# Windowed attention into a channel mix on one core: how the first batch's q and k come in, where its bias is added, how masks are stored, and a new order of all instructions

## The chip, the cores and the metric

The kernel runs on one core of one Trainium2 chip. The core has TensorE (PE, matrix products and transposes into PSUM), VectorE (DVE), ScalarE (ACT), GpSimd (POOL) and SyncE (SP). DMA transfers are issued here from SP (plain copies and transposing copies) and from POOL (copies that also cast fp32 to bf16). The metric is device time in microseconds (us), less is better; the time of a kernel is the median of its runs.

## The reference

q, k, v are fp32 arrays of 8 batches x 8 heads x 576 positions x 64. Attention is causal with a window of 128 positions and a linear distance bias per head; its result, with the heads side by side (512 columns), goes through a channel mix with a hidden width of 1024.

```
scores = scale * q @ k.T
bias   = slopes[h] * -(i - j)            # slopes 2^-1 ... 2^-8
mask   = (i - j >= 0) & (i - j < 128)
attn   = softmax(where(mask, scores + bias, -1e9));  y = attn @ v
x      = y as (batch, position, 512);  x_prev = x shifted by one position
xk = mu_k*x + (1-mu_k)*x_prev;  xr = mu_r*x + (1-mu_r)*x_prev
out = sigmoid(xr @ w_r) * (relu(xk @ w_k)**2 @ w_v)
```

Inputs and output are fp32; the kernel computes in bf16 with fp32 accumulation.

## The kernel before

**Units of work.** Heads are handled in pairs: pair `it` is batch `it // 4`, heads `2*(it%4)` and the next; there are 32. A pair has scores in two halves (`score.it.e`): the transposed k is the weight, and a half is one PSUM buffer of 2 heads x 512 columns that holds, for key blocks of 128, only the 256 query columns within reach. ACT takes the exponential of a half (`exp`), `av` multiplies by v with a column of ones beside it (so that it also gives the sum), DVE divides (`norm`), and the result is transposed (`ot`, `xt`) into x with channels on partitions. `xk` and `xr` are the two mixes. The channel mix works on column chunks of two batches (P = 0 to 3): `m1` (w_k), `rl` (relu on ACT), `kk` (square), `m2a`/`m2` (w_v, in two halves of the hidden width), `m3` (w_r), `rs` (tanh), `oo` (product) and `st` (store).

**Distance and mask.** For the pairs 0 to 3 (`EARLY`, batch 0) the bias is added in PSUM: two matmuls per half (line 206) multiply a scaled identity `sid` by the matrix of distances `dist` before the score's own matmuls add to it; positions outside the window have a distance of at least 2^20. For all other pairs the exponential is multiplied on DVE by a stored `mask` (line 246), which is the exponential of the bias, made on ACT from `dist` for two heads at a time (`mask0`). Both `dist` and `mask` hold 512 columns per head: 256 made directly, and 256 copied from them (`dcopy`, `mcopy`), in the layout of the second half of a pair.

**q and k of batch 0.** Pair 0's come in fp32 by two plain loads on SP (`lq`) and are cast on DVE (`c`, line 143), which also brings two heads beside each other. Pair 1's come by two casting loads on POOL (`lqp`), those of pairs 2 and 3 by two more (`lql`), and DVE reorders each pair (`ct`, line 157). Then PE transposes (`tq`, `tk`, line 166), and ACT copies q (`pq`) and DVE k (`pk`) out of PSUM. Batches 1 to 4 come by casting loads on POOL and `ct`; batches 5 to 7 are transposed by DMA (`tr`, `trt`).

**What sets the order.** Every operation is declared with its dependences, and the table `ORDER` names for each engine the order of its instructions. A small planner only interleaves these lists; each engine runs its own list strictly in order, and an instruction that waits holds all behind it. Rings bound how far one kind may run ahead: two score buffers (`sa`), four other PSUM buffers (`mm`), three relu buffers (`rl`). On POOL the loads and the clearing of buffers are one list, and the transfers behind its issues are served one after the other. PE starts with eight warm-up matmuls on zeros (line 190), and three more groups of 5, 2 and 3 (`fill`) stand in its list, the groups of 5 and 3 ahead of `tq.0`.

**Squares.** `kk` runs on DVE (line 341) except for two of the eight column groups of the hidden width in most chunks (`KFO`, `KCH`), 16 in all, which run on ACT (line 338).

Of the kernel before, what the change touches and what calls it, by code (L numbers as in the profile page):

```python
# [16 lines left out]
def kernel(  # L17
# [107 lines left out]

    def load_qp(g, i):
        nc.gpsimd.dma_start(
            out=ql_buf[0][:, g // 2, i, 2 * (g % 2):2 * (g % 2) + 2],
            in_=(q, k)[i][0, 2 * g:2 * g + 2, 0:SM].rearrange("h (p r) d -> p h (r d)", p=128))
# [57 lines left out]
    def warm(n):
        ps = p_mm.tile([128, 512], FP32, tag="mm", name="wm")
        for _ in range(n):
            nc.tensor.matmul(ps, lhsT=zero[:, 0:128], rhs=zero, start=True, stop=True)  # L190
# [4 lines left out]

    def scores(it, e):
# [4 lines left out]
        a0 = BASE[pieces[0][0]] + pieces[0][1] - 128 * pieces[0][0]  # L201
        w = sum(n for _, _, n in pieces)
        sa = T["sa", it, e] = p_sa.tile([128, 2, 512], FP32, tag="sa", name="sa")
        if early:
            for hl in range(2):
                nc.tensor.matmul(
                    sa[:, hl, 0:w] if e else sa[:, hl, 0:w].rearrange("p (u c) -> p u c", u=2),
                    lhsT=sid[:, 2 * g + hl],
                    rhs=dist if e else dist[:, None, 0:256].to_broadcast([128, 2, 256]),
                    start=True, stop=False, skip_group_check=True)  # L210
# [820 lines left out]
```

## Time and profile before

| | |
|---|---|
| time, three runs | 231.13 us median (230.84 to 231.31) |
| profiled execution, first to last instruction | 230.5 us |
| PE busy | 222.2 us (96%) |
| DVE busy | 192.2 us (83%) |
| ACT busy | 155.4 us (67%) |
| POOL busy | 88.7 us (38%) |
| chain that ended last, share on PE | 84% |
| DMA | 33.65 MB moved, mean 146 GB/s |

The page gives the span of one execution, and no other time for that execution; the runs' median is 0.6 us above that span. A line of a group or of the timeline reads: start, duration (in the timeline), engine, line of the kernel, operation, tile written <- tiles read, shapes, count, and in brackets how long the engine stood idle before it and what ended that. A busy PE is not a PE at its peak, since matmuls overlap and their ends are modelled.

### The profile page before, as it was taken

What the parts mean: (1) busy time and instruction counts of PE and PEld (TensorE: products, weight loads), DVE (VectorE), ACT (ScalarE), POOL (GpSimd) and SP (SyncE); (2) the same over time, 40 slices, a digit from 0 to 9 for tenths busy, and PEclk for the clock granted to TensorE, in tenths of its full rate; (3) what the DMA queues carried; (4) which work ended last, traced back from release to release, by engine and by line L of the source; (5) the groups of instructions that cost most, each with busy time, mean ns of one, the idle gap of its engine ahead of it and who ended that gap; (6) DMA issues with size and microseconds to landing.
All of it is one profiled execution on the core that took longest, in us unless ns stands there. A gap on an engine that the chain in (4) does not pass through costs nothing.

```text
span 230.5 us, 5326 instructions
## 1 busy us (share of the span) xinstructions
PE 222.2 (96%) x2099; PEld 130.0 (56%) x2099; DVE 192.2 (83%) x409; ACT 155.4 (67%) x265; POOL 88.7 (38%) x127
## 2 busy tenths in 40 slices
PE   7889899999999999999999999899999999999994
PEld 2446577855685565456657554455574555456653
DVE  7577999999998998999798996996876998985252
ACT  4299999985999998783789555685168744226700
POOL 8987857563897000697001954540000000000000
PEclk9999999999999999999999999999999999999999
DMA  6999999999999986999996999999954252413014
GB/s 137 160 173 187 198 177 192 195 180 162 177 155 161 154 120 100 123 128 204 120 256 144 166 120 156 203 176 197 134 128 119 79 163 77 102 46 141 0 67 162
DMA packets 117305, 33.65 MB, mean 146 GB/s; under 512 B 99608, under 2 KB 112928, under 8 KB 117280
## 3 DMA queue, kind: packets, MB, share of 16 engines
q0 software_dynamic: 83600, 16.52, 92.3%
q1 hardware_dynamic: 33680, 16.79, 34.1%
q8 instruction: 16, 0.26, 0.4%
q14 instruction: 9, 0.07, 0.1%
HBM read 33.56 MB, written 9.44 MB: 187 GB/s over the span
## 4 chain that ended last, share of the span: by engine, by line
PE 84%; ACT 7%; DMA 4%; DVE 2%; issue 1%; SPq 0%; DVEq 0%
PE pv L364 25%; PE ps L326 25%; PE pr L349 13%; PE sa L262 7%; PE sa L229 6%; DMA tt<-ts 4%; PE wm L190 3%; PE tp L166 3%; ACT at L237 3%; ACT qk L146 2%; PE pv L371 2%; ACT xt L287 1%; PE tp L282 1%; DVE qk L143 1%; ACT rl L332 1%
## 5 line engine op out<-in xcount | busy, mean ns | idle before, releaser
L237 ACT ACTIVATE at<-sa 128x1024 bf16<-128x1024 f32 x64 | 64.7, 1043 | 14.3 <-PE sa L229 14.2
L326 PE MATMUL ps<-xk,wk_sb 128*128 128x256 bf16 (+2 forms) x416 | 73.2, 314 | 0.5 <-DVE xk L315 0.4
L332 ACT ACTIVATE rl<-ps 128x256 bf16<-128x256 f32 (+2 forms) x104 | 46.3, 482 | 37.0 <-PE ps L326 30.0
L364 PE MATMUL pv<-wv_sb,kk 128*128 128x512 bf16 x272 | 65.3, 379 | 0.0
L326 PEld LDWEIGHTS <-wk_sb 128*128 128x128 bf16 x416 | 38.5, 98 | 24.1 <-issue 2.4
L364 PEld LDWEIGHTS <-kk 128*128 128x128 bf16 x272 | 25.5, 98 | 28.4 <-issue 1.3
L246 DVE TENSOR_TENSOR at<-at,mask 128x1024 bf16<-128x1024 bf16 x56 | 37.4, 684 | 1.9 <-ACT at L237 1.9
L118 POOL DMA_DIRECT2D vs<-in_v_dram x32 | 28.5, 897 | 26.3 <-PE sa L262 16.1
L341 DVE TENSOR_TENSOR kk<-rl 128x256 bf16<-128x256 bf16 (+2 forms) x88 | 28.0, 335 | 10.3 <-ACT rl L332 10.1
L349 PE MATMUL pr<-wr_sb,xr 128*128 128x512 bf16 x144 | 36.0, 379 | 0.0
L379 DVE SCALAR_TENSOR_TENSOR ot<-rs,pv 128x512 f32<-128x512 bf16 (+1 forms) x38 | 24.4, 653 | 7.4 <-PE pv L364 5.8
L315 DVE SCALAR_TENSOR_TENSOR xk<-dl,mu_sb,xt 128x576 bf16<-128x576 bf16 (+2 forms) x36 | 27.1, 752 | 1.3
L315 DVE SCALAR_TENSOR_TENSOR xr<-dl,mu_sb,xt 128x576 bf16<-128x576 bf16 x32 | 25.5, 812 | 0.0
L355 ACT ACTIVATE rs<-pr 128x512 bf16<-128x512 f32 x36 | 21.5, 608 | 4.9 <-PE pr L349 4.6
L262 PEld LDWEIGHTS <-at 128*128 128x128 bf16 x576 | 21.6, 98 | 5.3 <-issue 0.4
L274 DVE TENSOR_TENSOR xu<-sa,rc 128x640 bf16<-128x640 f32 x28 | 23.1, 824 | 1.2 <-DMA xt<-xu 0.3
L146 ACT COPY qk<-tp 128x1024 bf16<-128x1024 bf16 (+1 forms) x20 | 18.9, 960 | 5.6 <-PE tp L166 4.6
L349 PEld LDWEIGHTS <-xr 128*128 128x128 bf16 x144 | 13.2, 98 | 12.6 <-issue 0.4
L90 POOL DMA_DIRECT2D ql<-in_k_dram x12 | 10.9, 919 | 23.0 <-DVE ct L157 21.1
L262 PE MATMUL sa<-vs,at 128*128 128x65 bf16 x448 | 18.9, 194 | 0.0
L308 DVE TENSOR_TENSOR dl<-xt 128x576 bf16<-128x576 bf16 (+2 forms) x36 | 15.1, 420 | 3.2 <-DMA xt<-xu 2.1
L229 PE MATMUL sa<-qk 64*128 64x256 bf16 (+1 forms) x160 | 13.2, 259 | 0.8 <-ACT qk L146 0.5
(70 smaller groups left out, 207.6 us busy)
## 6 DMA issues: line engine op xcount, KB each, us to landing
out_dram<-ot SPq DMA_DIRECT2D x34, 256.0 KB, 3.6
vs<-in_v_dram POOLq DMA_DIRECT2D x32, 128.0 KB, 8.0
ql<-in_k_dram POOLq DMA_DIRECT2D x9, 256.0 KB, 6.7
ql<-in_q_dram POOLq DMA_DIRECT2D x9, 256.0 KB, 7.3
ql<-in_k_dram POOLq DMA_DIRECT2D x13, 128.0 KB, 6.5
ql<-in_q_dram POOLq DMA_DIRECT2D x13, 128.0 KB, 7.6
wk_sb<-in_moe_w_k_dram POOLq DMA_DIRECT2D x2, 512.0 KB, 9.0
wv_sb<-in_moe_w_v_dram POOLq DMA_DIRECT2D x2, 512.0 KB, 8.5
```

Source lines behind the costliest of these rows:

```text
L118: nc.gpsimd.dma_start(out=vs_buf[b % NLD][:, j, :, 0:D], in_=v[b, :, 128 * j:128 * j + 128, :].rearrange("h p d -> p h d"))
L229: nc.tensor.matmul(to, lhsT=kk_, rhs=qq_, start=not early, stop=True, skip_group_check=True)
L237: nc.scalar.activation(out=at_half(it, e), in_=T.pop(("sa", it, e)), func=AF.Exp, scale=float(scale))
L246: nc.vector.tensor_tensor(out=at, in0=at, in1=m, op=ALU.mult)
L262: nc.tensor.matmul(pa[:, hl, W * (t - t0):W * (t - t0) + W], lhsT=at[:, lo:lo + 128], rhs=vs[:, u, 2 * g + hl, :] if u < NF else tvb[:, 2 ...
L315: nc.vector.scalar_tensor_tensor(out=to, in0=T["dl", it][:, c0:c1], scalar=mu_sb[:, NPO * which + g:NPO * which + g + 1], in1=xp, op0=ALU. ...
L326: nc.tensor.matmul(ps[:, 0:c1 - c0], lhsT=wk_sb[:, po, 128 * fo:128 * fo + 128], rhs=xk[:, po, c0:c1], start=(po == 0), stop=(po == NPO - 1))
L332: nc.scalar.activation(out=rl[:, 0:c1 - c0], in_=T.pop(("ps", P, c0, fo))[:, 0:c1 - c0], func=AF.Relu, scale=RELU_SCALE)
L341: nc.vector.tensor_tensor(out=T["kk", P, c0][:, fo, 0:c1 - c0], in0=rl[:, 0:c1 - c0], in1=rl[:, 0:c1 - c0], op=ALU.mult)
L349: nc.tensor.matmul(pr, lhsT=T["xr", P][:, po, 128 * c:128 * c + 128], rhs=wr_sb[:, po], start=(po == 0), stop=(po == NPO - 1))
L364: nc.tensor.matmul(pv, lhsT=kk[:, fo, o:o + 128], rhs=wv_sb[:, fo], start=(fo == 0), stop=(fo == NFO - 1))
L379: nc.vector.scalar_tensor_tensor(out=T["ot", P, c][:, w0:w1], in0=T["rs", P, c][:, w0:w1], scalar=1.0, in1=pv[:, 0:w1 - w0], op0=ALU.add, ...
```

## The change

1. All eight loads of q and k of batch 0 are plain fp32 loads on SP (`lq`, `NHW = 4`), into both buffers that the DMA transposes use later. Each is cast once (`c`), straight into the order that the transposes read; three of the casts are on ACT, five on DVE. The four casting loads on POOL and the three `ct` of batch 0 go. q and k are transposed and copied apart for each of the four pairs.
2. The two bias matmuls of a half become an operation of their own (`bias`) with a place of its own in PE's list. It takes the score's PSUM buffer and waits for `sid` alone.
3. `dist` and `mask` hold 320 columns: 64 for distances counted from 0 on, and then the 256 as before. The second half reads them by a pattern whose rows overlap (`both`), and the copies `dcopy` and `mcopy` go. The key blocks of the second half lie in another order (`BASE`), and a block of padding columns behind each `at` buffer goes, with its memsets. A mask waits only for its own two heads' `mask0`.
4. `sid` is made on POOL, ahead of all loads there; the memsets and clears come ahead of the loads too.
5. The filler groups on PE are 2 and 2 instead of 5, 2 and 3.
6. The engine of an operation is read from `ORDER` (`flex`): 49 squares are on ACT instead of 16, of the PSUM copies of q and k `pq.0`, `pq.1`, `pq.2`, `pq.19` go to DVE and `pk.1` to ACT, `xt.0.0` and `xt.11` go to DVE, `tcopy.3` to ACT.
7. All five order lists are new. A branch that scaled x on ACT, used by no pair, is taken out.

```
-    KFO, KCH = (1, 5), ((0, 512), (0, 768), (1, 0), (1, 512), (1, 896), (2, 0), (2, 512), (2, 896))
-    XMUL = ()
-    NHW = 1
+    NHW = 4
...
-    ldr = qt_buf[-1].rearrange("p i j g c -> p (i j g c)").bitcast(FP32)[
-        :, 0:4 * NHW * NF * D].rearrange("p (i g h c) -> p i g h c", i=2, g=NHW, h=2)
+    ldr = [t.rearrange("p i j g c -> p (i j g c)").bitcast(FP32).rearrange(
+        "p (g i h c) -> p g i h c", g=2, i=2, h=2) for t in qt_buf]
+    cs0 = ql_buf[0].rearrange("p w i h c -> p (w i h c)").rearrange(
+        "p (g i r h d) -> p g i r h d", g=G, i=2, r=NF, h=2)
...
     def load_qk(g, i):
         nc.sync.dma_start(
-            out=ldr[:, i, g],
+            out=ldr[g // 2][:, g % 2, i],
...
     def cast_qk(g, i, f):
-        if i == 0:
-            T["cs", g] = csp.tile([128, 2, NF, 2, D], BF16, tag="ct", name="cs")
-        f(T["cs", g][:, i].rearrange("p r h d -> p h r d"),
-          ldr[:, i, g].rearrange("p h (r d) -> p h r d", d=D))
+        f(cs0[:, g, i].rearrange("p r h d -> p h r d"),
+          ldr[g // 2][:, g % 2, i].rearrange("p h (r d) -> p h r d", d=D))
...
-    BASE = (0, 256, 512, 768, 960)
+    BASE = (0, 256, 768, 576, 512)
...
+    LT = 64
+    NK = LT + 256
+
+    def both(t, o, step, n):
+        rows = t[:, 0].ap if n > 1 else t.ap
+        return bass.AP(t.tensor, t.offset + o, [list(rows[0]), [step, n], [LT, 2], [1, 256]])
+
+    def bias(it, e):
+        g = it % G
+        sa = T["sa", it, e] = p_sa.tile([128, 2, 512], FP32, tag="sa", name="sa")
+        for hl in range(2):
+            nc.tensor.matmul(
+                sa[:, hl].rearrange("p (u c) -> p u c", u=2),
+                lhsT=sid[:, 2 * g + hl],
+                rhs=both(dist, 0, 320, 1)[:, 0] if e else
+                dist[:, None, LT:].to_broadcast([128, 2, 256]),
+                start=True, stop=False, skip_group_check=True)
...
     def masked(it, e):
         g = it % G
-        at, m = at_half(it, e), mask[:, 2 * g:2 * g + 2]
+        at = at_half(it, e).rearrange("p h (u c) -> p h u c", u=2)
         if e == 0:
-            at = at.rearrange("p h (u c) -> p h u c", u=2)
-            m = m[:, :, None, 0:256].to_broadcast([128, 2, 2, 256])
+            m = mask[:, 2 * g:2 * g + 2, None, LT:].to_broadcast([128, 2, 2, 256])
+        else:
+            m = both(mask, 2 * g * NK, NK, 2)
...
     def square(P, c0, c1, fo):
-        if fo in KFO and (P, c0) in KCH:
+        if ENGOF.get(("kk", P, c0, fo)) == "ACT":
...
+        for c0, n in ((LT, 256), (0, LT)):
+            nc.gpsimd.iota(dist[:, c0:c0 + n], pattern=[[1, n]], base=0, channel_multiplier=-1,
+                           allow_small_or_imprecise_dtypes=True)
...
-    def make_sid(h):
-        nc.vector.tensor_scalar(out=sid[:, h], in0=ident,
+    def make_sid(h, eng):
+        eng.tensor_scalar(out=sid[:, h], in0=ident,
                                 scalar1=-(2.0 ** (-(h + 1))) / scale,
                                 scalar2=None, op0=ALU.mult)
...
+    def flex(name, eng, busy, run, deps=(), pri=0, alloc=None, uses=()):
+        eng = ENGOF.get(name, eng)
+        f = {"ACT": act_cast, "DVE": vec_cast, "POOL": pool_cast}[eng]
+        return op(name, eng, busy, lambda: run(f), deps, pri, alloc, uses)
...
-    FILL = (5, 2, 3)
+    FILL = (2, 2)
```

The beginnings of the new lists:

```
PE    tk.0 fill.0 fill.1 tq.0 tq.3 tk.3 bias.0.0 score.0.0 bias.3.0 tq.1 tk.1 tk.2 score.3.0 bias.1.0 tq.2
      bias.2.0 score.1.0 av.0.0 av.3.0 tmu score.2.0 tail.0 bias.2.1 score.2.1 ot.0.0 av.2.0 bias.3.1 av.1.0
      ot.3.0 score.3.1 ot.2.0 bias.0.1 ot.1.0 tq.7 bias.1.1 score.0.1 score.1.1 tq.5 tq.4 av.0.1 av.2.1 tail.1
      score.4.0 av.3.1 tq.6 ot.2.1 ot.0.1 score.7.0 av.1.1 ot.3.1 score.6.1 m1a.0.0.0 m1a.0.0.1 m1.0.0.0
      m1.0.0.2 m1.0.0.1 ot.1.1 score.5.0 m1.0.0.4 m1.0.0.6 m1.0.0.5 ...
ACT   mask0.6 mask0.2 c.0.0 c.3.1 mask0.4 pq.3 c.1.1 exp.0.0 pk.1 exp.3.0 mask0.0 exp.1.0 exp.2.0 exp.2.1
      exp.3.1 xt.3.0 xt.1.0 pq.7 exp.0.1 xt.2.0 pq.5 pq.4 exp.1.1 exp.4.0 pq.6 xt.2.1 xt.0.1 xt.3.1 exp.6.1
      exp.7.0 rl.0.0.2 xt.1.1 rl.0.0.0 rl.0.0.1 exp.5.0 ...
DVE   c.0.1 c.3.0 id8 pk.0 pq.0 c.1.0 pk.3 c.2.1 pq.1 c.2.0 pq.2 pk.2 norm.0.0 tcopy.0 norm.3.0 cmu xt.0.0 ...
POOL  sid ms clear clear0 lvs.0.0 lvs.0.1 lts.0.1 lts.0.0 lql.1.1.0 lql.1.1.1 lql.1.0.1 lql.1.0.0 lvs.0.4
      lvs.0.3 lvs.0.2 lts.1.1 lts.1.0 lts.2.0 lwk.0 lts.2.1 lwk.1 lvs.1.3 lql.2.1.1 lvs.1.0 lql.2.1.0 lvs.1.1
      lvs.1.4 lvs.1.2 lql.2.0.0 lql.2.0.1 lwr lql.3.1.1 lql.3.1.0 lts.3.0 lts.3.1 lwv.0 lwv.1 ...
SP    lq.0.1 lq.0.0 lq.3.0 lq.3.1 lq.1.0 lq.1.1 lq.2.1 lq.2.0 lmu.0 lmu.1 ...
```

More of the change, by code (lines that the diff above doesn't have):

```diff
@@ L200, in scores @@
         pieces = HALVES[e]
-        a0 = BASE[pieces[0][0]] + pieces[0][1] - 128 * pieces[0][0]
-        w = sum(n for _, _, n in pieces)
-        sa = T["sa", it, e] = p_sa.tile([128, 2, 512], FP32, tag="sa", name="sa")
+        a0 = 512 * e
         if early:
[L205 to L210, printed above, removed]
+            sa = T["sa", it, e]
+        else:
+            sa = T["sa", it, e] = p_sa.tile([128, 2, 512], FP32, tag="sa", name="sa")
         for (u, q0, n) in pieces:
@@ L906, in memsets_early @@
     def memsets_early():
-        for i in range(NAT):
-            nc.gpsimd.memset(at_buf[i][:, 2048:2112], 1.0)
         for i in range(2):
@@ L924, in add_qk @@
                [("tr", b - 2, 0), ("tr", b - 2, 1)] if b - 2 in CROSSED else
-               [("ct", G * (b - 2) + 2 * w + j) for j in range(2)]
-               if b > 2 or b == 2 and w else [], dma=dma[i], land=min(b, 2) * 700)
+               [("ct", G * (b - 2) + 2 * w + j) for j in range(2)] if b > 2 else
+               [(t, g) for t in ("tq", "tk") for g in range(2 * w, 2 * w + 2)] if b == 2 else [],
+               dma=dma[i], land=min(b, 2) * 700)
     def add_tails(b):
@@ L981 @@
         add_pair(it)
-    for i in range(2):
-        op(("mcopy", i), "DVE", (700, 270)[i], lambda i=i: copy_mask(i),
-           [("mask0", h) for h in range(0, H, 2)], 7 * G)
     for b in range(1, B):
```

471 lines of the change are left out of this document (215 added, 256 removed).

## The prediction

> **What bounds the kernel now.** I read the head of the page first, then the busy time by stretches.
>
> ```profile
> span 230.5 us, 5326 instructions
> PE 222.2 (96%) x2099; PEld 130.0 (56%) x2099; DVE 192.2 (83%) x409; ACT 155.4 (67%) x265; POOL 88.7 (38%) x127
> ```
>
> ```profile
> core 0: us, PE busy (x) PEld busy (x) DVE busy (x) ACT busy (x) POOL busy (x), PEclk, DMA share, GB/s
> 0.00:12.00 12.00, 9.97 (x51) 4.38 (x52) 7.70 (x26) 4.67 (x8) 11.07 (x27) 1.00 1.21 150
> 12.00:30.00 18.00, 16.06 (x232) 10.62 (x232) 15.00 (x43) 17.86 (x31) 14.85 (x25) 1.00 1.62 188
> 30.00:60.00 30.00, 29.90 (x339) 20.00 (x337) 29.69 (x65) 25.82 (x46) 17.63 (x24) 1.00 1.88 186
> 60.00:80.00 20.00, 20.00 (x231) 13.21 (x230) 18.44 (x40) 18.89 (x34) 13.39 (x16) 1.00 1.80 144
> 140.00:210.00 70.00, 69.21 (x546) 37.02 (x545) 59.62 (x115) 38.45 (x68) 6.81 (x8) 1.00 0.93 137
> ```
>
> From 30 us on PE hardly idles: 0.10 us to 60 and 0.79 in the stretch 140 to 210. Nothing large can be won there. The first 30 us are different: PE's 9.97 of 12 is mostly filler, ACT does 4.67 of 12 and then 17.86 of 18. So the opening is where time lies, and in it ACT, which is late to start and then full. The timeline of the opening, engine by engine:
>
> ```profile
> 1.19 6.44 PE L190 MATMUL wm<-zero 128*128 128x512 bf16 x16 [1.19 <-DVE zero L448]
> 7.47 0.39 PE L166 MATMUL tp<-ident,cs 128*128 128x128 bf16 x4
> 28.68 1.16 PE L326 MATMUL ps<-xk,wk_sb 128*128 128x256 bf16 x9
> ...
> 9.73 1.02 ACT L237 ACTIVATE at<-sa 128x1024 bf16<-128x1024 f32 x1 [1.25 <-PE sa L229]
> 16.34 1.93 ACT L237 ACTIVATE at<-sa 128x1024 bf16<-128x1024 f32 x2
> 26.32 1.06 ACT L146 COPY qk<-tp 128x1024 bf16<-128x1024 bf16 x1
> 27.21 1.09 ACT L237 ACTIVATE at<-sa 128x1024 bf16<-128x1024 f32 x1
> 28.75 0.49 ACT L332 ACTIVATE rl<-ps 128x256 bf16<-128x256 f32 x1
> ...
> 3.61 0.78 DVE L143 CAST cs<-qt 128x512 bf16<-128x512 f32 x1 [0.56 <-DMA qt<-in_q_dram]
> 4.38 0.60 DVE L143 CAST cs<-qt 128x512 bf16<-128x512 f32 x1
> 9.32 0.80 DVE L157 COPY ct<-ql 128x1024 bf16<-128x1024 bf16 x1
> ```
>
> The reader is to see three dates. The first transposes start at 7.47 though both casts were done by 5.0: sixteen fillers stood ahead of them. The second pair starts at 9.32, when its loads have come. The first relu starts at 28.75, and with it w_k's matmuls run without gaps (28.68). Ahead of that relu ACT runs eleven exps, the copies of seven pairs and eight copies of x.
>
> **The loads.** Here are size and landing of the second plain load, then POOL's queue: its second issue, the first load behind its opening memsets, the second half of w_k, w_v's issues; and the landing times of lines 138 (its first two), 436 and 441.
>
> ```profile
> qt<-in_k_dram SPq DMA_DIRECT2D x1, 256.0 KB, 3.1
> ...
> 2.24 0.76 POOL L138 DMA_DIRECT2D ql<-in_q_dram  x1
> 4.05 0.70 POOL L127 DMA_DIRECT2D ql<-in_k_dram  x1
> 17.65 0.74 POOL L436 DMA_DIRECT2D wk_sb<-in_moe_w_k_dram  x1 [0.78 <-DMA vs<-in_v_dram]
> L441 POOL DMA_DIRECT2D wv_sb<-in_moe_w_v_dram x2: 763/763/763, 34.3 to 36.3; - x2
> ...
> DMA to landing us min/median/max: 6.5/6.7/7.0
> DMA to landing us min/median/max: 8.5/9.0/9.6
> DMA to landing us min/median/max: 8.0/8.5/9.0
> ```
>
> The first plain load lands at 3.6 (the wait of its cast) and the second, 3.1 after its issue, by 4.38 (its cast starts without a wait): 0.75 apart. Eight of them in the new order (k0, q0, q3, k3, q1, k1, k2, q2) then land at 3.6, 4.35, 5.1, 5.85, 6.6, 7.35, 8.1, 8.85: the last one before pair 2 and 3's loads of now (2.24 + 7.0 = 9.24). On POOL, the queue now moves, between the landings at 9.24 and 17.65 + 9.6 = 27.25, the two loads of pair 1 (256 KB), batch 0's v and tails (704), batch 1's q, k and tails (1152) and w_k (1024): 3136 KB by the tiles' sizes in 18.0 us, 174 KB/us. On SP the two loads of mu now stand behind eight loads, three microseconds later; tmu, which wants them, is behind the first av.
>
> **POOL's new opening.** It issues no q or k of batch 0 (four issues of 0.7 to 0.9 us gone, 768 KB), but does a second iota, sid, the small memsets and all clears before its first load. Costs of groups by shape:
>
> ```profile
> L460 POOL MEMSET tt<- 128x256 bf16 x1 | 0.4, 394 | 0.0
> L908 POOL MEMSET at<- 128x64 bf16 x4 | 0.5, 208 | 0.0
> L428 ACT ACTIVATE mask<-dist 128x256 bf16<-128x256 bf16 x8 | 2.8, 408 | 0.6 <-DVE dist L415 0.6
> L146 ACT COPY qk<-tp 128x512 bf16<-128x512 bf16 x4 | 2.3, 584 | 4.9 <-PE tp L166 3.9 <-DVE qk L143 0.8
> L143 DVE COPY qk<-tp 128x512 bf16<-128x512 bf16 x4 | 2.8, 689 | 2.6 <-PE tp L166 2.5
> L338 ACT ACTIVATE kk<-rl 128x384 bf16<-128x384 bf16 x6 | 3.2, 538 | 0.0
> L341 DVE TENSOR_TENSOR kk<-rl 128x384 bf16<-128x384 bf16 x26 | 8.9, 352 | 7.1 <-ACT rl L332 7.0
> L246 DVE TENSOR_TENSOR at<-at,mask x56: 674/684/694, 32.6 to 192.0; 128x1024 bf16<-128x1024 bf16 x56
> ```
>
> A tensor_scalar on POOL does not occur. Nearest are its memsets, 208 ns for 64 columns and 394 for 256. Eight of 128 columns lie between 1.7 and 3.2 us; I take 2.5, and for an unknown stall up to double that. The clear of one batch takes the 1.05 us between 3.00 and 4.05; three of them and the small memsets make some 3.7 (estimate). So the first v load is issued at 1.5 + 2.5 + 3.7 = 7.7, say 8.0. It lands 2.9 us later (like a plain load) to 6.5 (like the first cast load); I take 4, so 12.0. Behind it, up to the second half of w_k, stand 2880 KB: 16.6 us at 174, so 28.6 against 27.25 now. For w_v's second half: 45.3 now; in the new order 3776 KB follow w_k, and between 27.25 and 45.3 the queue moved 3328 KB (184 KB/us), so 28.6 + 20.5 = 49.1. All weights come 1.4 to 3.8 us later than now; the price is what PE wants of them, below.
>
> [...]
>
> **The path to the first relu.** PE: eight warm-ups, tk.0, four fillers instead of ten. At the row's pace (1.19 to 7.47 for sixteen, 0.39 each, early ones slower) tq.0 starts at 6.7 instead of 7.47. DVE then runs pk.0, pq.0 (0.69 each, second done 7.9), c.1.0, pk.3, c.2.1, pq.1, c.2.0 (0.6 to 0.69 each) to 11.1, and pq.2, pk.2 to 12.9. ACT gets masks 6 and 2 (four activations; width 320 makes 408 at most 510 ns), c.0.0 at 4.4, c.3.1 at 5.85, pq.3 and c.1.1 (a cast on ACT has no row: the PSUM copy's 0.584 is nearest, 0.4 to 0.8 the bounds) and starts the first exp at 8.65 (9.73 now). The next ones follow at 10.25, 12.2 and, when pk.2 is done, 13.5: four exps end at 14.4, where the fourth now ends at about 17.3 (the pair at 16.34). score.2.1 needs tcopy.0, whose tail lands at about 13.6; exp.2.1 at 15.2. From there ACT has no wait: seven exps at 0.96, four copies at 0.89 (26.32 to 27.21) and six xt at about 0.3 make 12.3, first relu at **27.5** instead of 28.75. pq.6 is then done too.
>
> Does PE profit? Useful work by the chain's pieces:
>
> ```profile
> 34.82 0.45 PE tp L166 x8
> 39.25 0.55 PE sa L262 x18
> 47.62 3.45 PE pv L364 x16
> 51.07 0.55 PE sa L229 x12
> ```
>
> A pair's eight transposes are 0.45, its av 0.55, its two score halves 0.55, a 512-column matmul 0.216. Before 28.68 PE now has done seven pairs' transposes (3.15), sixteen bias matmuls (3.45), thirteen score halves (3.6), four av (2.2), tails and x transposes (1.55), one unit of w_k (0.43): 14.4. In the new list m1.0.0.4 is the first to want both a PSUM buffer behind the first relus (about 28.65) and w_k's second half (28.6). Ahead of it stand eight pairs' transposes (3.6), the same bias, av and tails, twelve halves (3.3) and three units (1.3): 15.4. PE is **1.0 us ahead** at the same date. Bias matmuls on their own cost nothing more: same sixteen, same width. They take the score's buffer earlier (there are two): bias.1.0 waits for the first exp (9.65), bias.2.0 for the second (11.2), and behind them on PE stand score.1.0 and score.2.0, whose operands come at 11.1 and 12.9 anyway; with earlier operands that wait would be the next one.
>
> **The rest.** 33 squares go from DVE to ACT (12 of 256, 12 of 384, 9 of 512 columns). On the row of 384: 352 off DVE, 538 on ACT; in all some 11 us less DVE, 17 us more ACT, hidden by ACT's 75 us of idle time, except that ACT has only 1.1 us free of 20 in 60 to 80. Two DVE copies of the masks and one of dist go. [...] Of PE's idle 0.89 us after 30 some may go and some may come, since every list is new: I take 0.2 saved, bounds 0.9 saved and 0.8 lost. The last units, products and stores keep their form, so the tail is the same.
>
> Sum: the profiled execution's 230.5 minus 1.0 minus 0.2 is 229.3. What lies around the span is not in the page; the median of the runs is 231.13, 0.6 more, so **229.9**.
>
> **Rivals.** *More gain.* POOL's opening at its lower bounds (1.7 for sid, 2.9 to land) brings w_k 1.9 us earlier, and relieved DVE lets PE follow: 229.9 - 1.9 = 228.0. For it: DVE's 29.69 of 30 in 30 to 60. Against it: ACT is as full.
>
> *Nothing gained.* The lead is taken back at w_v: m2a.0.1 comes about 17 us of PE work after m1.0.0.4, 45.6, and the first half lands at 46.3, the second at 49.1 against 48.3. PE in order waits 0.7 to 0.9 there: 231.0. Against it: PE would have to run that stretch at full density, which now it does not.
>
> *Slower, by POOL.* Sid on POOL at double (5 us) and 6.5 to the first landing put all cast loads 5 us later at the worst; I price 3 us. Then m1.0.0.4 waits for w_k until 31.6, PE cannot pass it, and 3.0 - 1.2 remain: 232.9; it decides from about 1.2 us late. For it: no row of such work on POOL, and no load is issued before sid. Against: the memset rows.
>
> *Slower, by ACT.* The moved squares fall into 30 to 80, where ACT has 5.3 us free (50 minus 44.71): some 5 us more work there delays relus, PSUM comes free late, PE waits 2 us: 231.9. Against: DVE loses as many squares.
>
> *Slower, by the clock.* Sixteen matmuls took 6.28 us at the start, where the later 0.216 would make 3.46: PE opens at about half pace. If with six fillers fewer it stayed so from 7 to 13.4, its 4.2 us of work there would take 8.4, 2 us too many: 231.9. [...]
>
> **Chances.** Forecast 0.40 (its own range 229.2 to 230.6), more gain 0.20, nothing gained 0.18, POOL 0.12, ACT 0.07, clock 0.03. 0.2% is 0.46 us, about what a measurement can tell from no change. Faster (below 230.67): 0.62, with a little of the others' edges; same 0.17; slower 0.21. The range goes from 227.6, a little past the larger gain, to 232.1, which holds the slower cases but half of POOL's.
>
> **What would show it.** Right: first exp near 8.7, first relu near 27.5, sid on POOL 2 to 3 us, second half of w_k landed by 29, PE without idle time after 32. Wrong: PE waiting on wk_sb or wv_sb (POOL), relus late behind squares (ACT), matmuls of 512 columns at 0.43 after 8 us (clock), masking multiplications above 0.7 us.

## The result, and the profile after

The changed kernel takes **243.69 us** (median of 4 runs, 241.58 to 244.05) against 231.01 (230.84 to 231.31) for the kernel before: ratio 1.0524, 95% interval 1.0482 to 1.0567. Forecast were 229.9 us and a range of 227.6 to 232.1. It is 12.7 us slower where 1.2 us faster was forecast. Some executions take over 1.5% longer than the fastest of the same kernel; the ratios below leave these out, the medians don't.

The head of the page of the changed kernel, and its chain that ended last (shares of the span by engine):

```profile
span 242.2 us, 5324 instructions
PE 224.5 (93%) x2093; PEld 131.5 (54%) x2093; DVE 184.4 (76%) x368; ACT 168.6 (70%) x297; POOL 90.8 (37%) x128
...
PE 62%; DMA 16%; POOL 9%; DVE 6%; ACT 3%; issue 2%; SPq 0%; POOLq 0%; DVEq 0%
```

PE is busy for 2.3 us more than before and the span is 11.7 us longer: the time went into waits of PE, and the chain now runs over DMA and POOL. The busy times by stretches, the stretches of the prediction and two short ones (the columns are stretch, length, the busy time of each engine with its instructions, granted clock, DMA share, GB/s):

```profile
0.00:12.00 12.00, 9.26 (x60) 4.22 (x60) 7.08 (x18) 8.43 (x16) 10.46 (x29) 1.00 0.55 175
12.00:30.00 18.00, 12.34 (x148) 7.83 (x148) 9.52 (x30) 10.08 (x14) 14.16 (x20) 0.77 1.90 150
30.00:60.00 30.00, 28.96 (x368) 20.65 (x367) 28.41 (x63) 29.34 (x52) 19.11 (x25) 0.97 1.79 182
60.00:80.00 20.00, 20.00 (x258) 13.97 (x251) 19.78 (x41) 18.74 (x35) 12.67 (x16) 1.00 1.95 143
80.00:140.00 60.00, 56.47 (x512) 30.74 (x511) 49.20 (x90) 41.82 (x69) 24.03 (x29) 1.00 1.45 159
140.00:210.00 70.00, 68.51 (x591) 37.29 (x590) 55.35 (x102) 48.49 (x88) 10.37 (x13) 1.00 0.97 128
...
12.00:16.00 4.00, 1.23 (x17) 0.71 (x16) 0.50 (x2) 1.30 (x2) 4.00 (x7) 0.86 1.68 107
16.00:20.00 4.00, 4.00 (x34) 2.15 (x32) 2.43 (x10) 2.05 (x2) 4.00 (x6) 0.50 1.29 161
```

Two stretches lost most. From 12 to 30 PE did 12.34 us of work (16.06 before), and at a granted clock of 0.77 (1.00 before). From 80 to 140 it did 56.47 of 60. The kernel before, in that second stretch and at its first `av`, which it reached at 14.30 without a wait:

```profile
80.00:140.00 60.00, 60.00 (x600) 34.28 (x598) 55.41 (x108) 43.16 (x69) 24.98 (x30) 1.00 1.46 152
...
14.30 0.53 PE L262 MATMUL pa<-vs,at 128*128 128x65 bf16 x12
```

From 12 to 30 PE, DVE and ACT are all idler than before: they wait for data. The timeline of the changed kernel, POOL, then ACT, then PE:

```profile
1.50 4.50 POOL L417 TENSOR_SCALAR sid<-ident 128x128 bf16<-128x128 bf16 x8 [0.18 <-DVE ident L404]
6.25 0.80 POOL L445 MEMSET tv<- 64x520 bf16 x1
10.10 1.96 POOL L118 DMA_DIRECT2D vs<-in_v_dram  x2
...
9.14 1.02 ACT L248 ACTIVATE at<-sa 128x1024 bf16<-128x1024 f32 x1
12.57 1.02 ACT L248 ACTIVATE at<-sa 128x1024 bf16<-128x1024 f32 x1 [0.29 <-PE sa L240]
35.24 0.39 ACT L332 ACTIVATE rl<-ps 128x256 bf16<-128x256 f32 x1
...
7.81 0.59 PE L205 MATMUL sa<-dist,sid 128*128 128x512 bf16 x2
13.79 0.27 PE L274 MATMUL pa<-vs,at 128*128 128x65 bf16 x3 [1.26 <-DMA vs<-in_v_dram]
15.57 0.66 PE L274 MATMUL pa<-vs,at 128*128 128x65 bf16 x9 [1.51 <-DMA vs<-in_v_dram]
17.31 1.06 PE L205 MATMUL sa<-dist,sid 128*128 128x512 bf16 x2
27.64 0.40 PE L274 MATMUL pa<-vs,at 128*128 128x65 bf16 x8 [1.97 <-DMA vs<-in_v_dram]
```

`sid` holds POOL for 4.50 us, the clears behind it for 4.0 more, and the first casting load of the whole kernel is issued at 10.10. The exps start at 9.14, 0.6 earlier than before, and soon have nothing to do: PE stands at `av` because v isn't there (waits of 1.26, 1.51 and 1.97 us), and from the second of these waits to 20 us the granted clock is half (0.50 in the row 16 to 20); two bias matmuls take 1.06 us there, at 17.31, and 0.59 at 7.81, where the clock is full. The first relu comes at 35.24, where it came at 28.75 before.

The second loss, at 88 us, again in the changed kernel's timeline (SP, then DVE and PE):

```profile
82.03 1.30 SPq L101 DMA_TRANSPOSE xt<-xu  x1
83.44 1.52 SPq L106 DMA_TRANSPOSE tt<-ts  x1
85.01 2.71 SPq L384 DMA_DIRECT2D out_dram<-ot  x4
...
91.11 0.69 DVE L379 SCALAR_TENSOR_TENSOR ot<-rs,pv 128x512 f32<-128x512 bf16 x1 [4.50 <-DMA out_dram<-ot]
...
91.85 1.02 PE L364 MATMUL pv<-wv_sb,kk 128*128 128x512 bf16 x4 [3.32 <-DVE ot L379]
```

Four products of the first chunks were ready by 69.7 us, in four buffers (`ot` has four). Their stores stand on SP's list behind `xt.12`, which waits for attention of batch 3, and behind `trt.5.1`; they are issued at 85.01. The fifth product has no buffer until one of them has landed: DVE stands 4.50 us at it, and PE 3.32 us behind DVE.

How the lag built up can be worked out from the matmul records, their columns added up at the 0.216 us that 512 take (16 in 3.45 us in the kernel before) and the fillers left out: for each amount of work, the time at which either kernel has done it. At 4 us of such work the changed kernel is 2.0 us **ahead**; at 12 us of work it is 5.9 behind, at 24 us 6.4, at 30 us 7.2, and from there to 68 us no more; at 70 us, behind the stall at 88, it is 10.5 behind, and 11.9 at the end.

### The profile page after: what moved, and what is told of

The parts are those of the page before. It is cut to its first block, busy times and chain, and to the rows that moved or that the text cites. A ratio compares the mean times of both kernels' runs of the same rounds, so it can differ in the third digit from the quotient of the medians.

```text
span 242.2 us, 5324 instructions
## 1 busy us (share of the span) xinstructions
PE 224.5 (93%) x2093; PEld 131.5 (54%) x2093; DVE 184.4 (76%) x368; ACT 168.6 (70%) x297; POOL 90.8 (37%) x128
## 4 chain that ended last, share of the span: by engine, by line
PE 62%; DMA 16%; POOL 9%; DVE 6%; ACT 3%; issue 2%; SPq 0%; POOLq 0%; DVEq 0%
PE ps L326 20%; PE pv L364 18%; PE pr L349 9%; PE sa L274 5%; PE sa L240 4%; DMA vs<-in_v_dram 4%; DMA ts<-in_q_dram 3%; DMA tt<-ts 3%; DMA xt<-xu 3%; POOL vs L118 3%; DMA out_dram<-ot 2%; POOL sid L417 2%; DVE at L258 2%; PE tp L164 2%; ACT at L248 2%
## 5 line engine op out<-in xcount | busy, mean ns | idle before, releaser
L248 ACT ACTIVATE at<-sa 128x1024 bf16<-128x1024 f32 x64 | 66.1, 1050 | 27.6 <-PE sa L240 27.4
L364 PE MATMUL pv<-wv_sb,kk 128*128 128x512 bf16 x272 | 66.0, 379 | 3.3 <-DVE ot L379 3.3
L332 ACT ACTIVATE rl<-ps 128x256 bf16<-128x256 f32 (+2 forms) x104 | 48.6, 487 | 26.9 <-PE ps L326 25.2
L349 PE MATMUL pr<-wr_sb,xr 128*128 128x512 bf16 x144 | 36.7, 379 | 0.0
L274 PEld LDWEIGHTS <-at 128*128 128x128 bf16 x576 | 22.4, 100 | 11.3 <-issue 5.1
L341 DVE TENSOR_TENSOR kk<-rl 128x256 bf16<-128x256 bf16 (+2 forms) x55 | 17.4, 328 | 14.6 <-ACT rl L332 14.6
L338 ACT ACTIVATE kk<-rl 128x256 bf16<-128x256 bf16 (+2 forms) x49 | 25.4, 526 | 0.3
L141 ACT COPY qk<-tp 128x1024 bf16<-128x1024 bf16 (+1 forms) x17 | 16.8, 999 | 0.7 <-PE tp L164 0.6
L122 POOL DMA_DIRECT2D tv<-in_v_dram x8 | 6.0, 756 | 27.8 <-PE sa L274 26.1
```

Source lines behind the costliest of these rows:

```text
L248: nc.scalar.activation(out=at_half(it, e), in_=T.pop(("sa", it, e)), func=AF.Exp, scale=float(scale))
L274: nc.tensor.matmul(pa[:, hl, W * (t - t0):W * (t - t0) + W], lhsT=at[:, lo:lo + 128], rhs=vs[:, u, 2 * g + hl, :] if u < NF else tvb[:, 2 ...
L332: nc.scalar.activation(out=rl[:, 0:c1 - c0], in_=T.pop(("ps", P, c0, fo))[:, 0:c1 - c0], func=AF.Relu, scale=RELU_SCALE)
L338: nc.scalar.activation(out=T["kk", P, c0][:, fo, 0:c1 - c0], in_=rl[:, 0:c1 - c0], func=AF.Square)
L349: nc.tensor.matmul(pr, lhsT=T["xr", P][:, po, 128 * c:128 * c + 128], rhs=wr_sb[:, po], start=(po == 0), stop=(po == NPO - 1))
L364: nc.tensor.matmul(pv, lhsT=kk[:, fo, o:o + 128], rhs=wv_sb[:, fo], start=(fo == 0), stop=(fo == NFO - 1))
```

## The experiments

The first theory after the result: **L**, casting loads late, by `sid` and the clears on POOL, is most of the loss; **O**, the new order is slow by itself and the late loads cost no more than the visible waits for v; **D**, `sid` on VectorE would delay the casts behind it; **S**, the stores wait on SP behind `xt.12`. Below, "ratio" is against the kernel before in the same series of runs. Most edits only move names in the order lists; three dots leave out names.

**1. `sid` back on VectorE** (e1_sid_dve).

```diff
 "POOL":
-    sid ms clear clear0 lvs.0.0 ...
+    ms clear clear0 lvs.0.0 ...
 "DVE":
-    c.0.1 c.3.0 id8 ...
+    c.0.1 sid c.3.0 id8 ...
```

> The changed kernel with one move: sid goes from the head of POOL's list to DVE's, behind its first cast, where DVE stands idle for 2.0 us. Theory L (late loads: what stands ahead of the first cast load on POOL, sid 4.5 us and the clears 4.0 us, is most of the loss): the first v load is issued 4 to 4.5 us earlier (near 5.8 instead of 10.1), w_k's second half lands near 29.5 instead of 33.7, the time falls by 4 us, to 239.5. Rival O (the new order is slow by itself, the loads only cost the two visible waits for v, 2.8 us): 241. Rival D (DVE now pays: sid delays the casts behind it): no gain, 243.5.

239.06 us, ratio 1.0306 (1.0239 to 1.0372): 2.2 points of the 5.2 are gone by one name. That is near theory L's figure for this move (239.5), and D falls. Its timeline, VectorE:

```profile
4.37 1.12 DVE L417 TENSOR_SCALAR sid<-ident 128x128 bf16<-128x128 bf16 x8
```

The same eight instructions take 1.12 us in all on VectorE and 4.50 on POOL.

**2. The clears behind the first loads as well** (e2_sid_clear).

```diff
 "POOL":
-    ms clear clear0 lvs.0.0 lvs.0.1 lts.0.1 lts.0.0 lql.1.1.0 ... lwk.1 lvs.1.3 ...
+    clear0 lvs.0.0 lvs.0.1 lts.0.1 lts.0.0 ms lql.1.1.0 ... lwk.1 clear lvs.1.3 ...
```

> As the run with sid on DVE, and on POOL the clears of batches 1 and 2 go behind w_k's second half and the small memsets behind the first tails, so that only the clear of batch 0 is ahead of the first load. Theory L: the first v load is issued near 2.8, w_k's second half lands near 26.5, and the lag that PE has from 24 us on (7.5 us against the kernel of before) goes: 236.5. Rival O: as much as with sid alone, 239.5 to 241, because the new lists were made for later loads. The clock row of 12 to 30 us is 1.00 again by theory L, since PE's pauses were waits for v.

238.43 us, ratio 1.0288 (1.022 to 1.0355), hardly less than without it; theory L had 236.5, so its part on the clears falls. The first v load was issued 2.4 us earlier than in experiment 1 (2.55 against 4.97) and landed 1.1 us earlier (11.03 against 12.16): it took 8.5 us instead of 7.2, while the eight plain loads came in.

**3. The stores of the first chunks ahead of `xt.12`** (e3_stores), POOL as in the changed kernel.

```diff
 "SP":
-    ... lmu.0 lmu.1 xt.12 trt.5.1 st.0.1 st.0.2 st.0.0 st.0.3 trt.5.0 ...
+    ... lmu.0 lmu.1 st.0.1 st.0.0 st.0.3 st.0.2 xt.12 trt.5.1 trt.5.0 ...
```

> The changed kernel with one move on SP: the first four stores stand ahead of xt.12 and trt.5.1 instead of behind them. Theory S (DVE's product oo.0.4 waits 4.5 us for a store that waits on SP for xt.12, and PE waits 3.3 us behind it): the wait at 87 us goes, and the time falls by 3.3 us to 240.3. Rival: the pause is made up later or comes back at another place, since PE is not the only full engine: less than 1 us, 242.8.

239.52 us, ratio 1.0366 (1.0318 to 1.0414). The stretch 80 to 140 of this kernel, to be held against 56.47 above:

```profile
80.00:140.00 60.00, 59.42 (x550) 33.34 (x558) 53.40 (x97) 43.56 (x75) 27.89 (x34) 1.00 1.68 155
```

PE does 2.95 us more there, and 1.6 points of the ratio (3.6 us) are gone.

**4. All three moves** (e4_all).

> The three moves together (sid to DVE, clears behind w_k, first stores ahead of xt.12). If the losses are separate and add up: 7 + 3.3 us less than the changed kernel, 233. If they overlap (PE late by one is not late by the other): 236. If the new parts themselves (plain loads, one cast, bias apart, overlapping masks) gain the 1.2 us that I forecast, less than 1 us is left to the tail transposes' wait, and the time is 230 to 231.

235.11 us, ratio 1.0161 (1.0121 to 1.0202). The parts nearly add up: 2.2, 0.2 and 1.6 points by themselves, 3.6 together. 1.6 points are left. The traced execution took 238.50 us at a mean granted clock of 0.986, the other three 234.08 to 235.26 at 0.992 to 1.000. Two things stand out in the traced one:

```profile
12.00:16.00 4.00, 3.04 (x23) 1.14 (x20) 1.92 (x4) 1.97 (x4) 3.12 (x4) 0.67 1.46 195
16.00:20.00 4.00, 4.00 (x38) 2.26 (x36) 2.21 (x9) 2.59 (x3) 1.97 (x3) 0.50 2.85 152
...
141.25 0.21 PE L240 MATMUL sa<-tt,qt 64*128 64x64 bf16 x2 [1.84 <-DMA tt<-ts]
```

Its clock falls to half behind three waits of PE for casts (0.93 us ahead of 8.15, 0.95 ahead of 11.51, 0.96 ahead of 13.73), and at 141 us PE waits for a tail of batch 6. The next three experiments start from this kernel.

**5. Those three waits filled with matmuls on zeros** (e5_pads).

```diff
         tp = T["tp", it, t0] = p_mm.tile([128, 1024], BF16, tag="mm", name="tp")
+        for _ in range({(3, 1): 4, (2, 1): 4, (2, 0): 4}.get((it, t0), 0)):
+            nc.tensor.matmul(tp.bitcast(FP32), lhsT=zero[:, 0:128], rhs=zero, start=True, stop=True)
```

> All three list moves, and in the three places of the opening where TensorE waited 0.9 to 1.0 us for a cast (ahead of tk.3, tk.2 and tq.2) four 512-column matmuls on zeros, 2.6 us of filler in all, written into the PSUM tile that the transposes then overwrite. Clock theory: with the three moves alone the granted clock was 0.67 from 12 to 16 us and 0.50 from 16 to 20, right behind those waits, and TensorE's 7.0 us of work there took some 3 us more than at full clock; with the waits filled the clock stays at 1.00 and the time falls from 235.1 to 232 to 233. Load theory (what is left is late operands): the clock may rise, but TensorE then only waits longer, 235. Squares theory (ScalarE full from 30 to 60 us): 235.

236.06 us, ratio 1.0216 (1.0167 to 1.0265): no faster. The same two stretches:

```profile
12.00:16.00 4.00, 4.00 (x43) 2.06 (x41) 1.89 (x6) 2.53 (x5) 3.17 (x5) 1.00 1.50 194
16.00:20.00 4.00, 4.00 (x58) 2.51 (x55) 3.56 (x14) 3.50 (x5) 2.25 (x4) 1.00 2.61 157
```

The clock stays at 1.00, so the fillers did what they were for, and still the time isn't lower. The clock theory falls, as a cause of the time that is left. Experiment 4 itself says the same: its execution with a mean granted clock of 1.000 took 234.08 us, still 3.2 us more than the kernel before.

**6. The tail of batch 6's q loaded earlier** (e6_tail).

```diff
 "POOL":
-    ... lqn.6.1.3 lts.6.1 lqn.5.0.0 ... lvs.5.1 lts.6.0 lvs.7.1 ...
+    ... lqn.6.1.3 lts.6.1 lts.6.0 lqn.5.0.0 ... lvs.5.1 lvs.7.1 ...
```

> All three list moves, and on GpSimd's list lts.6.0 (the tail of batch 6's q) right behind lts.6.1, ahead of ten other loads, so that its transpose on SyncE is not waited for: TensorE's wait for tt at 141 us was 1.84 us against 0.79 in the kernel before. Tail theory: that wait goes, 234.0 against 235.1. If the stretch behind it is bound by other work, 235.

232.75 us, ratio 1.0071 (1.0046 to 1.0096). That is 0.9 points (2.1 us) less, where 1.1 us were expected; in its trace no wait for `tt` is left.

**7. Four of the moved squares back on VectorE** (e7_squares; from experiment 4).

```diff
 "ACT":
-    ... kk.0.0.6 ... kk.0.256.2 ... kk.0.256.5 ... kk.0.256.3 ...
 "DVE":
+    ... kk.0.0.6 mask.6.1 ... kk.0.256.2 kk.0.256.3 kk.0.256.5 mask.11.0 ...
```

> All three list moves, and four of the moved squares of the first two chunks (kk.0.0.6, kk.0.256.2, .3, .5) back from ScalarE to VectorE, some 1.6 us less on ScalarE and 1.1 us more on VectorE between 35 and 60 us. Squares theory: ScalarE, busy 30.00 of 30 us there, is what holds TensorE; 233.5 to 234. Otherwise VectorE (29.07 of 30) takes the same delay: 235 or a little more.

234.55 us, ratio 1.0133 (1.0068 to 1.0199), an interval that overlaps that of experiment 4: inconclusive, and taken up again in experiment 10.

**8. The kernel before with fewer fillers, and nothing else** (e8_fill).

```diff
-    FILL = (5, 2, 3)
+    FILL = (1, 2, 1)
```

> The kernel before with four filler matmuls ahead of tq.0 and tk.0 in place of ten, and nothing else: the early start of the opening by itself. By the prediction's reasoning (an earlier first pair moves ScalarE and the first relu ahead, 1 us) 230.0. Load theory: the second pair lands at 9.24 in any case, and TensorE only waits there: 231. Clock theory: less filler leaves TensorE waiting, the clock falls to one half behind the wait, and the time is 232 or more.

231.40 us, ratio 1.0013 (0.999 to 1.0037): no change. PE and ACT in the opening of this kernel:

```profile
9.50 1.15 PE L166 MATMUL tp<-ident,ct 128*128 128x128 bf16 x16 [1.87 <-DVE ct L157]
...
7.52 1.02 ACT L237 ACTIVATE at<-sa 128x1024 bf16<-128x1024 f32 x1 [1.25 <-PE sa L229]
28.56 0.50 ACT L332 ACTIVATE rl<-ps 128x256 bf16<-128x256 f32 x1
```

The first exp comes 2.2 us earlier than before (7.52 against 9.73), PE then waits 1.87 us for the second pair, and the first relu comes 0.19 us earlier (28.56 against 28.75). An earlier start of the first pair is worth next to nothing to the first relu.

**9. The kernel before with `sid` alone on POOL** (e12_before_sid).

```diff
 "DVE":
-    dcopy c.0.0 id8 c.0.1 sid pk.0 ...
+    dcopy c.0.0 id8 c.0.1 pk.0 ...
 "POOL":
-    lql.0.1.1 lql.0.1.0 clear0 ...
+    sid lql.0.1.1 lql.0.1.0 clear0 ...
...
-        nc.vector.tensor_scalar(out=sid[:, h], in0=ident,
+        nc.gpsimd.tensor_scalar(out=sid[:, h], in0=ident,
...
-    op(("sid",), "DVE", 970, ...
+    op(("sid",), "POOL", 970, ...
```

> The kernel before with sid alone moved from VectorE to the head of GpSimd's list, ahead of all its loads. Queue theory: eight tensor_scalar take 4.5 us there as in the changed kernel, every casting load comes 4 to 4.5 us later, and the time is 234.5 to 235.5. If the cost in the changed kernel came from its other lists (plain loads, TensorE's order) and not from sid itself: 231.5 to 232.5.

236.19 us, ratio 1.0222 (1.0179 to 1.0266): 5.1 us for one operation of 1.1 us moved off a busy engine. POOL, PE and ACT, and one stretch:

```profile
1.50 4.72 POOL L422 TENSOR_SCALAR sid<-ident 128x128 bf16<-128x128 bf16 x8 [0.33 <-DVE ident L405]
...
12.66 1.89 PE L166 MATMUL tp<-ident,ct 128*128 128x128 bf16 x16 [4.03 <-DVE ct L157]
14.34 1.06 PE L206 MATMUL sa<-dist,sid 128*128 128x512 bf16 x2
...
32.89 0.50 ACT L332 ACTIVATE rl<-ps 128x256 bf16<-128x256 f32 x1
...
12.00:16.00 4.00, 3.34 (x23) 2.10 (x24) 2.88 (x7) 1.54 (x4) 4.00 (x12) 0.50 1.70 128
```

The first load on POOL is issued 4.9 us later, the pair that PE waits for lands 2.9 us later (12.07 against 9.22) and w_k's second half 5.1 us later; PE stands 4.03 us, and the first relu is 4.1 us late. `sid` at the head of POOL's list has the same price in a kernel that has nothing else of the change: 2.2 points, as much as experiment 1 won back by undoing it, though here PE waits for q and k and in the changed kernel for v.

**10. The squares again, from experiment 6** (e13_tail_squares): the edits of 6 and 7 together.

> The four list moves, and four of the squares moved to ScalarE (kk.0.0.6, kk.0.256.2, .3, .5) back on VectorE. Squares theory: with nothing else late any more, ScalarE (28.90 of 30 busy from 30 to 60 us with the four moves) is what holds TensorE, and the time falls by 0.8 or more, to the kernel before or under it (231). Opening theory: what is left of the loss (0.7%) was made before 30 us, and the time stays at 1.007 of before.

232.86 us, ratio 1.0079 (1.005 to 1.0108), the same as without it (1.0071). The squares theory falls for these four of the 33 moved squares; the others were not tried.

**11. Experiment 6 with the clears ahead of the loads again** (e14_tail_clears).

```diff
 "POOL":
-    clear0 lvs.0.0 lvs.0.1 lts.0.1 lts.0.0 ms lql.1.1.0 ... lwk.1 clear lvs.1.3 ...
+    ms clear clear0 lvs.0.0 lvs.0.1 lts.0.1 lts.0.0 lql.1.1.0 ... lwk.1 lvs.1.3 ...
```

> Three of the four list moves: the clears stay ahead of the loads on GpSimd (first v load issued near 5 us, not 2.55). Opening theory in the form that casting loads and the eight plain loads take each other's time: the last plain load lands at 10.6 in place of 11.3 to 13.1, v some 1.5 us later, and the time is 1.007 to 1.010 of before, the same within 0.5 us as with the clears moved. If an early v load is worth its 2.4 us: 1.015 or more.

232.93 us, ratio 1.0068 (1.0046 to 1.0089): the same as experiment 6. So three names in three lists (`sid`, four stores as one group, `lts.6.0`) hold 4.6 of the 5.2 points. Its traced execution, at 231.16 us the fastest of twelve (231.16 to 233.41), shows an opening near the forecast one, ACT and then PE:

```profile
9.12 1.02 ACT L248 ACTIVATE at<-sa 128x1024 bf16<-128x1024 f32 x1
28.09 0.44 ACT L332 ACTIVATE rl<-ps 128x256 bf16<-128x256 f32 x1
...
21.82 0.40 PE L274 MATMUL pa<-vs,at 128*128 128x65 bf16 x8 [1.83 <-DMA vs<-in_v_dram]
```

The plain loads landed some 0.75 us apart up to 9.96, v from 11.05 on, the second half of w_k at 27.84. Experiment 1 has the same lists up to there, and in its trace these dates are 10.87, 12.16 and 30.22, and the first relu comes at 30.45 instead of 28.09. So the same lists gave openings 1 to 2.4 us apart in these two executions.

**12 and 13. The wait for v that is left.** e9_v_first (from experiment 6) and e15_v_first_all (from 11) take batch 0's last three v loads ahead of two loads of batch 1; the second moves what depends on these on three engines too.

```diff
 "POOL":
-    ... lql.1.1.1 lql.1.0.1 lql.1.0.0 lvs.0.4 lvs.0.3 lvs.0.2 lts.1.1 ...
+    ... lql.1.1.1 lvs.0.4 lvs.0.3 lvs.0.2 lql.1.0.1 lql.1.0.0 lts.1.1 ...
 # e15_v_first_all, in place of e9's tq.5 tq.4 behind av.2.1:
 "PE":  tq.5 tq.4 av.0.1 -> av.0.1 tq.5 tq.4
 "DVE": ct.5 ct.4 ... norm.0.1 -> ... norm.0.1 ct.5 ct.4
 "ACT": pq.5 pq.4 exp.1.1 -> exp.1.1 pq.5 pq.4
```

> The four list moves (sid, clears, stores, tail of batch 6), and batch 0's last three v loads on GpSimd's list ahead of two loads of batch 1 (lql.1.0.1, lql.1.0.0), as in the kernel before; on TensorE tq.5 and tq.4 behind av.2.1. TensorE waited 1.84 us there for v (22.8 us), and the stretch 20 to 30 held 7.29 us of TensorE work against 8.85 before. Order theory: what is left of the loss (232.75 against 231.2) is this wait, and the time comes to 231 to 231.5. If w_k, landing at 28.9 in any case, takes the wait over: 232.5.

> Three moves (sid on VectorE, stores ahead of xt.12, tail of batch 6's q early; the clears ahead of the loads), and batch 0's last three v loads ahead of lql.1.0.1 and lql.1.0.0 on GpSimd's list, this time with everything that stood behind those two loads moved with them: on TensorE av.0.1 ahead of tq.5 and tq.4, on VectorE norm.0.1 ahead of ct.5 and ct.4, on ScalarE exp.1.1 ahead of pq.5 and pq.4. With the loads alone moved, TensorE's wait for v went and one of 1.94 us for xu took its place, because VectorE stood at ct.5. Opening theory: the 1.83 us wait for v at 21.8 us is what is left of the loss; the time is 231.0 to 231.7. If the loads of batch 1 that now come later are wanted as soon, the wait only moves to them: 232.9 or more.

236.17 us, ratio 1.0217 (1.0173 to 1.0261), and 233.90 us, ratio 1.0115 (1.0061 to 1.0169). The first is 3.4 us slower than experiment 6, which neither of its two expectations had; in its trace the wait for v is gone, and PE waits 1.94 us for a division (`xu`) instead. The second is not faster than experiment 11 (1.0068); the two intervals overlap. In its trace:

```profile
22.25 1.89 PE L164 MATMUL tp<-ident,ct 128*128 128x128 bf16 x16 [1.64 <-DVE ct L155]
```

The wait for v has become a wait for batch 1's q and k. Whichever goes first, the other is late. That would fit a stretch bound by how fast casting loads arrive, but these two runs don't show it.

**14. Half of the plain loads undone** (e10_cast, from experiment 6): q and k of pairs 1 and 2 by casting loads at the head of POOL's list.

```diff
+        if g in (1, 2):
+            nc.gpsimd.dma_start(
+                out=staged(g, i),
+                in_=(q, k)[i][0, 2 * g:2 * g + 2, 0:SM].rearrange("h (p r) d -> p h (r d)", p=128))
+            return
 "POOL":
-    clear0 lvs.0.0 ...
+    lq.1.0 lq.1.1 lq.2.1 lq.2.0 clear0 lvs.0.0 ...
```

> The four list moves, and q and k of pairs 1 and 2 by casting loads at the head of GpSimd's list, ahead of its first clear, in place of plain loads on SyncE; the four copies to the token order read bf16. So a part of the change undone: four of eight plain loads. If plain loads are the cheaper ones (six of them alone landed 0.75 us apart, where casting loads of the same rows come 1.0 to 1.4 apart), v and w_k come 2 us later and the time is 234.5. If the plain loads hold the casting ones back by as much as they save, 232.5 to 233.

234.23 us, ratio 1.0136 (1.0094 to 1.0179), 0.65 points worse: no run was under 234.02, where experiment 6 had none over 233.11. The first v load is issued at 5.57 there instead of 2.55, but that by itself cost nothing in experiment 11 (5.03). So the plain loads are a gain, within these lists.

**15. The one late wait of the kernel before** (e11_before_tail).

```diff
 "POOL":
-    ... lqn.6.1.0 lvs.5.4 ... lvs.7.1 lts.6.0 lts.6.1 lvs.6.0 ...
+    ... lqn.6.1.0 lts.6.0 lts.6.1 lvs.5.4 ... lvs.7.1 lvs.6.0 ...
 "SP":
-    ... tr.6.1 tr.6.0 xt.17 ... xt.20 trt.6.0 trt.6.1 xt.21 ...
+    ... tr.6.1 tr.6.0 trt.6.0 trt.6.1 xt.17 ... xt.20 xt.21 ...
```

> The kernel before with the loads of batch 6's tails (lts.6.0, lts.6.1) ahead of lvs.5.4 on GpSimd's list and their two transposes (trt.6.0, trt.6.1) right behind tr.6.0 on SyncE's: the one wait of TensorE that is left after 30 us in the kernel before (0.79 us for tt at 145.71) is taken away. Tail theory: 230.4. If the stretch is bound otherwise: 231.2.

232.92 and 233.36 us in two executions, 237.66 and 238.66 in the other two, beside 231.07 (230.05 to 232.14): every run was above all of the kernel before's, and neither expectation had that. The wait for `tt` is gone and another stands in its place, at 134 us:

```profile
134.21 0.39 PE L229 MATMUL sa<-qt 64*128 64x256 bf16 x4 [1.32 <-DVE xu L274]
```

What delays that division was not followed further; a wait that can be taken away is not yet time that can be won.

**What stays open** is the last 0.7% (1.6 us). The wait for v at 21.82 (1.83 us) is of that size, but the execution that has it took 231.16 us, no more than the kernel before's median of 231.17, so the wait by itself doesn't make the loss. More telling is the first relu: 28.09 in that execution, 29.09 in experiment 10's (232.98 us) and 29.34 in experiment 6's (232.41 us). w_k's second half landed at 27.84, 28.80 and 28.88 in these, ahead of the relu each time. Why loads land at other times from one execution to another was not tested. By their medians, no version of the changed kernel here reaches the kernel before.

## Why the prediction was wrong, step by step

Two steps failed: the price of POOL's new opening, with v's landing left out of the sum, and the small allowance for the new lists. The gain that the sum rested on, PE 1.0 us ahead at the first relu, came out as PE some 6 us behind.

**The step that failed first: "POOL's new opening".** It took 2.5 us for `sid`, between 1.7 and 3.2 by POOL's memsets; measured were 4.50. The memsets (208 and 394 ns) said too little of it: seven of the eight instructions take 522 to 532 ns, one 709. With the clears (3.7 taken, 4.0 measured, right) the first v load is issued at 10.10, not 8.0. Its landing was taken at 4 us behind that; measured 3.65.

**"174 KB/us" for the queue** was the second size in that step. The 2880 KB up to w_k's second half took from 13.75 to 33.69: 144 KB/us, and w_k is 5.1 us later than the forecast 28.6. With `sid` on VectorE and the same loads in the same order the same 2880 KB took from 12.16 to 30.22 in experiment 1, 159 KB/us, and from 11.05 to 27.84 in experiment 11, 172 KB/us, near the forecast. Why the queue is slower in the changed kernel wasn't tested.

**The rival "Slower, by POOL" was the mechanism, with a price far too low** (232.9). It had `sid` at 5 us, near the 4.50 measured, let all casting loads come late, and then looked at w_k alone ("m1.0.0.4 waits for w_k until 31.6"). But batch 0's v is behind `sid` too, and `av` wants it at 12.5 us, so PE lost 4.7 us in three waits for v before w_k was needed at all. Nor was v's date put against the exps in the sum: "first v load issued 8.0, landing at 12.0" was used as the start of the queue and never as an operand. `sid` cost 5.0 us (experiment 1) and 5.1 us (experiment 9); the rival's chance of 0.12 was too small for a cost whose nearest row was of another kind.

**"The path to the first relu"** was too early, and its lead is worth less than taken. First exp: 8.65 forecast, 9.14 measured (the plain loads came 0.75 us apart, as taken, but a microsecond later, the last at 9.8 and not 8.85). With `sid` off POOL the first relu came at 28.09 at best (experiment 11; 27.5 forecast, 28.75 in the kernel before) and between 29.09 and 32.23 in experiments 1, 2, 4 to 7 and 10. And a lead in the first exps doesn't reach the end: in the kernel before, 2.2 us at the first exp were 0.19 at the first relu and nothing in the time (experiment 8). The gain of 1.0 us rested on such a lead.

**Lists that were not read.** The prediction said of the new order lists "since every list is new: I take 0.2 saved, bounds 0.9 saved and 0.8 lost". Two misplaced names cost more than that bound: the stores behind `xt.12` 3.6 us (experiment 3) and `lts.6.0`, which stands twelve loads behind `lts.6.1`, 2.1 us (experiments 4 and 6). The first could have been found in the diff: the ring of four `ot` buffers, the four stores, and ahead of them on SP an instruction that needs attention of batch 3. What stands behind a waiting instruction was followed on POOL and on PE, and on SP only for mu.

**The clock.** The rival priced a half clock by fewer fillers at 2 us and a chance of 0.03. The chance was the author's estimate: no run here shows how long PE has to pause before the clock falls. The opening up to 12 us ran at 1.00 with the fewer fillers (two bias matmuls took 0.59 us at 7.81), so that rival did not come; the clock fell later, to 0.77 from 12 to 30, behind waits for v that the forecast didn't have. After a single wait of 4.03 us the clock was 0.50 (experiment 9), but behind three waits of 0.93 to 0.96 us with work between them it was 0.50 as well (experiment 4), and behind one of 1.46 us it was 0.63 from 24 to 28 us (experiment 2), while one of 1.83 us left it at 1.00 (experiment 11). So the length of the longest wait doesn't settle it. In experiment 5 the clock was held at 1.00 and the time was no lower: in that version the half clock was not what the time hung on. What the half clock cost in the changed kernel itself was not measured apart.

**Squares and masks.** "Slower, by ACT" did not come: the four squares that were moved back change nothing (experiment 10). Masking by overlapping rows costs nothing: 683 ns on the mean, where line 246 took 674 to 694 before. Line 258 of the changed kernel:

```profile
L258 DVE TENSOR_TENSOR at<-at,mask 128x1024 bf16<-128x1024 bf16 x56 | 37.2, 683 | 0.2 <-ACT at L248 0.2
```

**"Nothing gained"**, w_v late: its second half landed at 54.24 (49.1 forecast), 5.1 us late like w_k's, and PE was late too; no wait for it appears.

**The base.** The prediction put 0.6 us around the span, the difference of a traced span (230.5) and a median (231.13). In every later execution for which both numbers are known, time is 1.7 to 1.8 us over span (231.18 with a span of 229.4 for the kernel before). So the traced execution was most likely one of about 232.3 us. The forecast was a difference, and isn't touched by it; but one wait of 0.79 us in it was taken as a property of the kernel, and removing it (experiment 15) gained nothing.

## What to carry to other kernels

POOL, which issues these loads, had hardly any free time at its start (11.07 us busy of the first 12 in the kernel before). Price what is put ahead of its first load by the delay of every operand behind it, the first one wanted and not the largest one. Before a new order list is believed, walk each queue for instructions that wait long and ask what stands behind them, above all stores that free a small ring. A lead early in an opening is worth little while a later operand comes when it came before (experiment 8: 2.2 us at the first exp, 0.19 at the first relu). And one trace is one execution: see where it lies among the others before a date in it is held against a forecast.

## What the runs showed of the hardware that was not expected

- A tensor_scalar of 128x128 bf16 takes 522 to 532 ns on POOL in the changed kernel (one 709), the next one starts 0.5 to 0.7 us after its start, and 8 take 4.50 us; on VectorE 8 take 1.12 us (experiment 1).
- Where POOL and VectorE worked side by side, POOL's instruction grew in few cases: in the changed kernel 532, 532, 527, 527 ns beside VectorE's bounding of `dist` and in the pause behind it, and 709 beside a fp32 cast; in experiment 9 688 and 707 beside two such casts. The lengthening of 0.16 to 0.18 us beside the casts isn't what made `sid` 4.50 us, since the other seven took 522 to 532 ns each and make up most of it; where it comes from was not tested.
- Where plain loads and casting loads were under way together, each took longer to land. Eight plain loads by themselves had landed by 9.8 in the changed kernel (10.6 in experiment 3); with casting loads issued from 2.55 us on (experiments 2, 4 to 7, 10 and 12), the last plain load landed between 11.3 and 13.1, and the first casting load 7.4 to 8.9 us after its issue (3.65 when it came after them). Why, no run here shows.
